# Decode attention over a 512 MiB cache: K and V loaded by pairs of heads instead of single heads

## The chip, the cores and the metric

The kernel runs on one core of a Trainium2 chip. The metric is the device time of one execution in microseconds. A core has TensorE (PE, matrix products into PSUM), VectorE (DVE), ScalarE (ACT), GpSimd (POOL) and SyncE (SP), which issues most transfers here. A transfer (DMA) is issued by SP or ACT and carried out by 16 DMA engines, each of which takes its share of the rows. The engines run on their own and wait for each other through semaphores. SBUF has 128 partitions; a transfer into it writes one row into each.

## What is computed

One token for each of four batch entries goes through an attention block with a stored cache and then a gated MLP:

```
x: [4, 1, 512] bf16            h  = x + Attn(layernorm(x))
k_cache, v_cache: [4, 32, 8192, 128] bf16   (256 MiB each)
q = (x @ wq) per head          wq: [512, 4096]
p = softmax(q . k / sqrt(128)) over 8192 keys
o = p . v                      wo: [4096, 512]
h2 = h + (sigmoid(g) * u) @ w_down,  g = ln(h) @ w_gate,  u = ln(h) @ w_up   (F = 1792)
```

There are 4 x 32 = 128 (batch, head) pairs, called heads here. Each reads 2 MiB of K and 2 MiB of V once. All inputs together are 550.8 MB.

## The kernel before

**Loading.** `KV` holds NSL = 8 slots, each of 64 x 128 bf16 values per partition: 16 KB per partition, 2 MiB in all. `k_src` and `v_src` give partition p the 64 consecutive keys 64p to 64p + 63 of one head, so a row of a transfer is 16 KB. The list `order` (L321 to L331) says which load follows which: K of head 0 in four pieces (128 rows of 4 KB), the query weights in four pieces (rows of 8 KB), then K heads; four pieces of the output weights (rows of 1 KB) come between K 2 and K 5, and from head 9 on K n and V n - 9 alternate (LAGH = 9). The gate weights stand before V of head 125, the up and down weights at the end. The last V is in four pieces again. All loads are issued by SP in this order. `take_slot` gives slots in turn; SP waits until the load that held the slot is used up: for K until its last transpose (`t_tr`), for V until its last product (`t_pv`). `pump` issues a load as soon as that point has been written into the program.

**Scores.** K arrives with keys on partitions and must be turned. A head is worked in four chunks of 16 keys per partition. For each chunk, `transposes` (L369) turns 32x32 blocks of 32-bit words on DVE into one of NKT = 4 buffers `kTc`, and `scores` (L383) runs four matmuls of 512 columns against `Lq`, a window that holds the head's query so that its scores land on their own rows of a PSUM bank. `q_windows` fills such windows from `q2`. Eight heads (GH = 8) times four chunks times four fill the 128 rows of one bank: a group, of which there are 16.

**Softmax.** When a group's scores are complete, `softmax` (L400) takes the row maximum on DVE, and hands four steps, p1 to p4, to the list `chain`. They find each head's maximum, take the exponent on ACT with a running sum, divide, and write the probabilities into `PT` with a 32x32 transpose on DVE. They are written into the program at fixed distances, so that other work stands between them.

**Output.** `pv` (L445) has the probabilities as the stationary 32 columns and V as the moving 512, four matmuls on four column strips at once, summed in a bank per group. `finish` (L498) copies the bank to SBUF on ACT, picks the wanted strips by four matmuls against `selq`, and `project` (L482) multiplies by the output weights and adds to the residual `sth`. The last group is worked otherwise: V is stationary and the moving operand is one column, 512 small matmuls (L473), so that no selection follows.

**Order of work.** The main loop (L553) counts chunks u. At each it writes the transposes of chunk u, due steps of `chain`, the scores of chunk u - 1, and one chunk of `pv` 36 chunks back, so that PE alternates four score matmuls with four output matmuls. `q_projection` (L520) stands after the first four transposes and has one step for each piece of the query weights.

**The end.** After the last `pv` come the projection, the second layernorm, gate and up products (L597), the sigmoid, the down product in two halves (L613), a transpose back and the store of 4 KB.

```
for n in range(NH):
    order.append((4 * n, 0, "k", n))
    order.append((4 * (n + LAGH), 1, "v", n))
```

Of the kernel before, what the change touches and what calls it, by code (L numbers as in the profile page):

```python
# [11 lines left out]
NSL = 8  # L12
NKT = 4
LAGH = 9
GH = 8

# [60 lines left out]
def bass_sequential_preLN__mha_block_cached__glu_gated_glu__decode_kernel(  # L77
# [18 lines left out]
    R = S // 128  # L96
    NK = R // 4
    RC = R // 4
    QH = 2
    NH = B * H  # L100
    NG = NH // GH
    SCALE = float(DH) ** -0.5
# [6 lines left out]
    with ExitStack() as es:  # L109
# [21 lines left out]
        Lq = SB("Lq", [128, 2, QH, 4, W], BF16)  # L131
# [3 lines left out]
        PT = SB("PT", [128, 2, NK * GH * 32], BF16)  # L135
# [37 lines left out]
        keys = ["sp", "act", "dve", "pool", "pe", "x", "out", "wg", "wu", "wd0", "wd1"]  # L173
        keys += [f"sl{i}" for i in range(NSL)] + [f"k0p{i}" for i in range(4)] + [f"vl{i}" for i in range(4)]
        keys += [f"wq{i}" for i in range(4)] + [f"wo{i}" for i in range(4)]
# [13 lines left out]
        t_lq0 = emit("pool", lambda e: e.memset(Lq[:, :, :, :, :], 0.0))  # L189
# [3 lines left out]
        t_x = prog.dma("sp", "x", lambda e: e.dma_start(x_bf[:, :], A_x.rearrange("b s d -> (b s) d")))  # L193
# [30 lines left out]
        def f_xT(e):  # L224
            ins = None
            for c in range(NDC):
                ins = e.matmul(cols(bank[XO], c), x_bf[:, 128 * c:128 * (c + 1)], ident[0:B, 0:B],
                               start=True, stop=True)
            return ins
        t_xT = emit("pe", f_xT, [t_x, t_ident])  # L230
        t_xTc = emit("dve", lambda e: e.tensor_copy(stx[:, 0:NDC * B], bank[XO][:, 0:NDC * B]), [t_xT])
        t_h = emit("dve", lambda e: e.tensor_copy(sth[:, 0:NDC * B], bank[XO][:, 0:NDC * B]), [t_xT])
        t_xn, t_xst = layernorm(stx, t_xTc, 0, xnT, bank[XS], None)
        t_m8 = emit("dve", lambda e: e.tensor_reduce(
            M8[:, :], identf[:, :].rearrange("p (t i) -> p i t", i=GH), AX.X, ALU.max), [t_identf])
# [3 lines left out]
            Gmat[:, :].rearrange("p (t i) -> p t i", i=GH),  # L239
            bass.AP(raw(M8), 0, [[GH, 128], [0, 16], [1, GH]])), [t_m8])  # L240
# [15 lines left out]
        sp_jobs = []  # L256

        def k_src(n):
            b, h = n % B, n // B
            return A_k_cache[b, h, :, :].rearrange("(p r) d -> p (r d)", p=128)  # L260

        def v_src(n):
            b, h = n % B, n // B
            return A_v_cache[b, h, :, :].rearrange("(p r) d -> p (r d)", p=128)

        QN = R * 128 // 4
# [20 lines left out]
        def emit_head(kind, n, src, done, pieces):  # L287
            slot, w = take_slot((kind, n))
            if pieces:
                done[n] = [prog.dma("sp", f"{pieces}{s}", lambda e, s=s: e.dma_start(  # L290
                    KV[:, slot, QN * s:QN * (s + 1)], src[:, QN * s:QN * (s + 1)]), w) for s in range(4)]
                return
            done[n] = [prog.dma("sp", f"sl{slot}", lambda e: e.dma_start(KV[:, slot, :], src), w)] * 4  # L293

        def emit_weight(kind):
            slot, w = take_slot((kind, 0))
            if kind == "wd":
                wd_v = in_slot(slot, [[D, NFT], [1, D]])
                src = B_w_down.rearrange("(t p) f -> p t f", p=128)
                half = NFT // 2  # L300
                t_w[kind] = (wd_v, [prog.dma("sp", f"wd{i}", lambda e, i=i: e.dma_start(
                    wd_v[:, half * i:half * (i + 1), :], src[:, half * i:half * (i + 1), :]), w) for i in range(2)])
                return
# [4 lines left out]
        def emit_wq():  # L308
            src = A_wq.rearrange("(c p) f -> p c f", p=128)
            for c in range(NDC):  # L310
                t_wq.append(prog.dma("sp", f"wq{c}", lambda e, c=c: e.dma_start(wq_v[:, c, :], src[:, c, :])))  # L311
# [4 lines left out]
        def emit_wo(i):  # L316
            src = A_wo.rearrange("(h p) f -> p h f", p=128)
            t_wo.append(prog.dma("sp", f"wo{i}", lambda e: e.dma_start(  # L318
                wo_v[:, 8 * i:8 * (i + 1), :], src[:, 8 * i:8 * (i + 1), :]), [t_qproj[0]]))

        order = []  # L321
        for n in range(NH):
            order.append((4 * n, 0, "k", n))
            order.append((4 * (n + LAGH), 1, "v", n))
        order.sort()
        order = [(k, n) for _, _, k, n in order]
        order.insert(1, ("wq", 0))
        for i, after in enumerate((2, 3, 4, 5)):
            order.insert(order.index(("k", after)) + 1, ("wo", i))
        order.insert(order.index(("v", NH - 3)), ("wg", 0))  # L330
        order += [("wu", 0), ("wd", 0)]  # L331
# [8 lines left out]
        def pump():  # L340
            while next_dma[0] < len(order) and ready(*order[next_dma[0]]):
                kind, n = order[next_dma[0]]
                next_dma[0] += 1
                if kind == "k":
                    emit_head("k", n, k_src(n), t_k, "k0p" if n == 0 else "")
                elif kind == "v":
                    emit_head("v", n, v_src(n), t_v, "vl" if n == NH - 1 else "")
                elif kind == "wq":
                    emit_wq()
                elif kind == "wo":  # L350
                    emit_wo(n)
                else:
                    emit_weight(kind)
# [15 lines left out]
        def transposes(n, s):  # L369
            u = 4 * n + s  # L370
            slot = slot_of["k", n]
            t_copy[u] = emit("dve", lambda e: e.transpose(  # L372
                kTc[:, u % NKT, :], KVW[:, slot, 64 * RC * s:64 * RC * (s + 1)]), [t_k[n][s], t_score.get(u - NKT)])
            if s == 3:
# [5 lines left out]
        def scores(u):  # L380
            n, s = u // 4, u % 4
            g, i = n // GH, n % GH
            first = i == 0 and s == 0  # L383
            last = i == GH - 1 and s == 3
            off = 31 - (GH * s + i)
            k3 = kTb[:, u % NKT, :].rearrange("p (r c i e) -> p r c i e", c=2, i=32, e=2)

            def f(e):
                ins = None
                for ce in range(4):  # L390
                    ins = e.matmul(sbank(g), Lq[:, n // QH % 2, n % QH, ce, off:off + 128],  # L391
                                   k3[:, :, ce // 2, :, ce % 2], start=first and ce == 0, stop=last and ce == 3)
                return ins
            w = [t_copy[u], t_lq[n // QH]]
# [6 lines left out]
        def softmax(g):  # L401

            t_mx = emit("dve", lambda e: e.tensor_reduce(mpart[:, :], sbank(g), AX.X, ALU.max),  # L403
                        [t_score[32 * g + 31], st_.get("p1")])
            box = {}

            def p1():
# [5 lines left out]
                    mrow[0:1, :], bank[XS][0:1, 0:128].rearrange("p (k i) -> p i k", i=GH), AX.X, ALU.max),  # L413
                    [box["p1"]])
                box["d2"] = emit("dve", lambda e: e.tensor_copy(  # L415
                    rowpad[0:1, :].rearrange("p (k i) -> p k i", i=GH),
                    bass.AP(raw(mrow), 0, [[GH, 1], [0, 16], [1, GH]])), [d2, t_rp0])
# [19 lines left out]
            def p4():  # L437
                pb = g % 2
                dst = bass.AP(raw(PT), pb * NK * GH * 32, [[2 * NK * GH * 32, 128], [GH * 32, NK], [1, 4], [36, GH]])
                t_ptc[g] = emit("dve", lambda e: e.transpose(dst, E_sb[:, :]),  # L440
                                [box["d4"], t_pt0, t_pvg.get(g - 2)])
            return [(4, p1), (6, p2), (9, p3), (13, p4)]

        def pcol(g, i, rr):
            return g % 2, (rr * GH + i) * 32  # L445

        def pv(n, m):
            g, i = n // GH, n % GH
            first = i == 0 and m == 0
            last = i == GH - 1 and m == 3  # L450
            slot = slot_of["v", n]
            w = [t_v[n][m], t_ptc[g]]
            if first and g > 1:
                w.append(t_oev[g - 2])
            if g < NG - 1:
                def f(e):
                    mms = []
                    for j in range(4):
                        rr = 4 * m + j
                        pb, o = pcol(g, i, rr)  # L460
                        mms.append(e.matmul(obank(g)[32 * j:32 * (j + 1), :], PT[:, pb, o:o + 32],  # L461
                                            in_slot(slot, [[RC * 128, 4], [1, 128]], rr * 128),
                                            start=first, stop=last, tile_position=(0, 32 * j)))
                    return mms if last else mms[-1]
                tok = emit("pe", f, w, incs=4 if last else 1)
            else:
                def f(e):
                    ins = None
                    for r in range(16 * m, 16 * (m + 1)):
                        q = r // RC  # L470
                        pb, o = pcol(g, i, r % RC)
                        o += 4 * i + q
                        ins = e.matmul(obank(g)[:, i:i + 1], KV[:, slot, 128 * r:128 * (r + 1)],  # L473
                                       PT[:, pb, o:o + 1], start=(r == 0), stop=(r == R - 1))
                    return ins
                tok = emit("pe", f, w)
            if m == 3:
# [20 lines left out]
        def finish(g):  # L498
# [5 lines left out]
            def s1():  # L504
                def f(e):
                    ins = None
                    for q in range(4):
                        ins = e.matmul(bank[XO][:, 0:GH], O_sb[:, 128 * q:128 * (q + 1)],  # L508
                                       selq[:, q:q + 29:4], start=(q == 0), stop=(q == 3))
# [8 lines left out]
            return [(4, s1), (6, s2)]  # L518

        def q_projection():  # L520
            for c in range(NDC):
                def f(e, c=c):
                    ins = None
# [4 lines left out]
                    return ins  # L528
                t = emit("pe", f, [t_wq[c], t_xn, t_xTc])
# [12 lines left out]
            q_windows(0)  # L542
            q_windows(1)

        def q_windows(k):
            dst = bass.AP(raw(Lq), k % 2 * QH * 4 * W + 31, [[2 * QH * 4 * W, 128], [4 * W, QH], [W, 4], [32, 4]])
            src = bass.AP(raw(q2), QH * k, [[4 * NH, 128], [1, QH], [NH, 4], [0, 4]])
            keep = bass.AP(raw(amask), 0, [[4, 128], [0, QH], [0, 4], [1, 4]])
            t_lq[k] = emit("dve", lambda e: e.tensor_tensor(dst, src, keep, ALU.mult),  # L549
                           [st_["q"], t_lq0, t_am, t_score.get(4 * QH * (k - 1) - 1)])  # L550


# [128 lines left out]
```

## Time and profile before

| | us |
|---|---|
| median of 3 runs | 1307.28 (1306.99 to 1307.47) |
| the profiled execution | 1307.25 |
| its span in the profile | 1305.1 |
| PE busy (matmul) | 883.7 |
| DVE busy | 682.3 |
| ACT busy | 27.4 |
| DMA, mean over the span | 423 GB/s |
| issue to landing, K head | 33.9 |
| DVE's waits for K | 445.1 |

The profile is of one execution. Busy times are sums over instructions; a share of the span is not a share of the path. "PE" lines are matmuls and "PEld" the loads of their stationary operand; "SPq" is SP's issuing of a transfer. The slices cut the span into 40 equal parts with one digit of busy share each. In a list of waits a line says who waited, for whom, the sum in us, how often, and the longest. In a timeline a line says start, duration, engine, line of the kernel, operation, what it writes and reads, how many, and in brackets how long the engine had been idle and what released it.

### The profile page before, as it was taken

To read this page: it belongs to the slowest core of one execution; us is meant where nothing else is said; L and a number is where in the kernel's file an instruction comes from. 1 tells how busy PE (TensorE), PEld (TensorE's weight loads), DVE (VectorE), ACT (ScalarE), POOL (GpSimd) and SP (SyncE) were. 2 spreads that over 40 slices of the span, in tenths; PEclk is the share of its full clock that TensorE was granted. 3 is DMA by queue.
4 is the path that set the end of the run, shared out by engine and by line. 5 is a ranking of instruction groups with operands and counts; after the bars stand their busy time and mean duration, and the time that the engine had idled before them with its cause. 6 is when DMAs were issued, how large, how long until landed. Compare 5 with 4: busy or idle time off the path is not lost.

```text
span 1305.1 us, 11528 instructions
## 1 busy us (share of the span) xinstructions
PE 883.7 (68%) x5133; PEld 283.5 (22%) x5133; DVE 682.3 (52%) x750; ACT 27.4 (2%) x55; POOL 10.3 (1%) x11
## 2 busy tenths in 40 slices
PE   4675776777667676676677667676667767667654
PEld 2121221222112121221212112121221212112133
DVE  6675554645546555554645546554554645545420
ACT  0000000000000000000000000000000000000000
POOL 3000000000000000000000000000000000000000
PEclk9888788787888888788888888888888888888865
DMA  9999999999999999999999999999999999999997
GB/s 373 407 426 428 428 427 427 427 428 428 427 430 426 428 429 427 427 428 427 428 427 428 429 427 429 426 428 428 426 429 429 425 429 428 427 428 426 428 423 306
DMA packets 45433, 551.52 MB, mean 423 GB/s; under 512 B 4420, under 2 KB 10312, under 8 KB 12360
## 3 DMA queue, kind: packets, MB, share of 16 engines
q1 hardware_dynamic: 45384, 550.79, 99.8%
q8 instruction: 40, 0.66, 0.2%
q14 instruction: 9, 0.07, 0.0%
HBM read 550.77 MB, written 0.00 MB: 422 GB/s over the span
## 4 chain that ended last, share of the span: by engine, by line
DMA 84%; PE 13%; SPq 2%; DVE 0%; issue 0%
DMA KV<-in_A_v_cache_dram 80%; PE PS L391 9%; PE PS L461 4%; DMA KV<-in_A_k_cache_dram 1%; DMA KV<-in_B_w_down_dram 1%; SPq L293 1%; DMA Wreg<-in_A_wq_dram 1%; SPq L318 0%; DVE kTc L372 0%; SPq L311 0%; SPq L290 0%; PE PS L473 0%; PE PS L525 0%; PE PS L613 0%; SPq L193 0%
## 5 line engine op out<-in xcount | busy, mean ns | idle before, releaser
L372 DVE STREAM_TRANSPOSE kTc<-KV 128x1024 f32<-128x1024 f32 x512 | 606.1, 1225 | 446.0 <-DMA KV<-in_A_k_cache_dram 445.1
L391 PE MATMUL PS<-kTc,Lq 128*128 128x512 bf16 x2048 | 650.8, 448 | 14.5 <-DVE kTc L372 12.6
L461 PE MATMUL PS<-KV,PT 128*32 128x512 bf16 x1920 | 224.4, 458 | 335.0 <-DMA KV<-in_A_v_cache_dram 335.0
L391 PEld LDWEIGHTS PS<-kTc,Lq 128*128 128x128 bf16 x2048 | 181.4, 109 | 330.1 <-issue 209.1
L461 PEld LDWEIGHTS PS<-KV,PT 128*32 128x32 bf16 x1920 | 50.2, 95 | 594.8 <-DMA KV<-in_A_v_cache_dram 386.9
L549 DVE TENSOR_TENSOR Lq<-q,amask 128x32 bf16<-128x32 bf16 x64 | 18.1, 285 | 41.1 <-PE PS L391 40.8
L440 DVE STREAM_TRANSPOSE PT<-E_sb 128x512 bf16<-128x512 bf16 x16 | 37.3, 2333 | 0.0
L425 ACT ACTIVATE E_sb<-PS,negmb 128x512 bf16<-128x512 f32 x16 | 11.0, 688 | 1153.8 <-DVE negmb L423 1153.8
L473 PE MATMUL PS<-PT,KV 128*128 128x1 bf16 x512 | 15.2, 165 | 20.1 <-DMA KV<-in_A_v_cache_dram 19.9
L508 PE MATMUL PS<-selq,O_sb 128*128 128x8 f32 x120 | 16.7, 266 | 11.7 <-ACT O_sb L500 11.7
L412 DVE TENSOR_REDUCE mrow<-PS 1x8 f32<-1x128 f32 x16 | 4.4, 276 | 31.8 <-PE PS L408 31.8
L508 PEld LDWEIGHTS PS<-selq,O_sb 128*128 128x128 f32 x120 | 15.3, 200 | 16.6 <-ACT O_sb L500 16.6
L473 PEld LDWEIGHTS PS<-PT,KV 128*128 128x128 bf16 x512 | 14.4, 104 | 20.8 <-DMA KV<-in_A_v_cache_dram 20.6
L585 DVE CAST OT<-PS 128x8 bf16<-128x8 f32 x1 | 0.2, 167 | 35.0 <-PE PS L473 35.0
L420 PE MATMUL PS<-identf,rowpad 128*128 128x1 f32 x32 | 8.1, 322 | 10.5 <-DVE rowpad L415 10.5
L403 DVE TENSOR_REDUCE mpart<-PS 128x1 f32<-128x512 f32 x16 | 10.9, 683 | 7.2 <-PE PS L391 7.2
L433 DVE RECIPROCAL rsum<-PS 128x1 f32<-128x1 f32 x16 | 2.7, 168 | 21.8 <-PE PS L431 21.8
L525 PE MATMUL PS<-xnT,Wreg 128*128 128x4 bf16 x128 | 4.0, 167 | 12.8 <-DMA Wreg<-in_A_wq_dram 12.8
L500 ACT ACTIVATE O_sb<-PS 128x512 f32<-128x512 f32 x15 | 9.0, 597 | 73.7 <-PE PS L461 73.7
L420 PEld LDWEIGHTS PS<-identf,rowpad 128*128 128x128 f32 x32 | 6.7, 261 | 16.6 <-DVE rowpad L415 16.6
L431 PEld LDWEIGHTS PS<-sig,Gmat 128*128 128x128 f32 x32 | 7.9, 305 | 7.6 <-issue 6.1
L431 PE MATMUL PS<-sig,Gmat 128*128 128x1 f32 x32 | 9.0, 351 | 0.7 <-ACT E_sb L425 0.7
(66 smaller groups left out, 97.2 us busy)
## 6 DMA issues: line engine op xcount, KB each, us to landing
KV<-in_A_k_cache_dram SPq DMA_DIRECT2D x127, 2048.0 KB, 33.9
KV<-in_A_v_cache_dram SPq DMA_DIRECT2D x127, 2048.0 KB, 33.3
Wreg<-in_A_wq_dram SPq DMA_DIRECT2D x4, 1024.0 KB, 11.8
Wreg<-in_A_wo_dram SPq DMA_DIRECT2D x4, 1024.0 KB, 15.0
KV<-in_A_k_cache_dram SPq DMA_DIRECT2D x4, 512.0 KB, 5.7
KV<-in_A_v_cache_dram SPq DMA_DIRECT2D x4, 512.0 KB, 27.5
KV<-in_B_w_gate_dram SPq DMA_DIRECT2D x1, 1792.0 KB, 34.5
KV<-in_B_w_up_dram SPq DMA_DIRECT2D x1, 1792.0 KB, 26.0
```

The lines of the kernel that those rows point to most:

```text
L293: done[n] = [prog.dma("sp", f"sl{slot}", lambda e: e.dma_start(KV[:, slot, :], src), w)] * 4
L372: t_copy[u] = emit("dve", lambda e: e.transpose(kTc[:, u % NKT, :], KVW[:, slot, 64 * RC * s:64 * RC * (s + 1)]), [t_k[n][s], t_score.get( ...
L391: ins = e.matmul(sbank(g), Lq[:, n // QH % 2, n % QH, ce, off:off + 128], k3[:, :, ce // 2, :, ce % 2], start=first and ce == 0, stop=last ...
L403: t_mx = emit("dve", lambda e: e.tensor_reduce(mpart[:, :], sbank(g), AX.X, ALU.max), [t_score[32 * g + 31], st_.get("p1")])
L420: t = emit("pe", lambda e: e.matmul(bank[XS][:, 128:129], rowpad[:, :], identf[:, 0:1], start=True, stop=True), [box["d2"], t_rp0])
L425: box["a2"] = emit("act", lambda e: e.activation(E_sb[:, :], sbank(g), ACT.Exp, bias=negmb[:, 0:1], scale=SCALE, accum_out=sig[:, 0:1]), [ ...
L431: t = emit("pe", lambda e: e.matmul(bank[XS][:, 130:131], Gmat[:, :], sig[:, 0:1], start=True, stop=True), [box["a2"], t_gm])
L440: t_ptc[g] = emit("dve", lambda e: e.transpose(dst, E_sb[:, :]), [box["d4"], t_pt0, t_pvg.get(g - 2)])
L461: mms.append(e.matmul(obank(g)[32 * j:32 * (j + 1), :], PT[:, pb, o:o + 32], in_slot(slot, [[RC * 128, 4], [1, 128]], rr * 128), start=fir ...
L473: ins = e.matmul(obank(g)[:, i:i + 1], KV[:, slot, 128 * r:128 * (r + 1)], PT[:, pb, o:o + 1], start=(r == 0), stop=(r == R - 1))
L508: ins = e.matmul(bank[XO][:, 0:GH], O_sb[:, 128 * q:128 * (q + 1)], selq[:, q:q + 29:4], start=(q == 0), stop=(q == 3))
L549: t_lq[k] = emit("dve", lambda e: e.tensor_tensor(dst, src, keep, ALU.mult), [st_["q"], t_lq0, t_am, t_score.get(4 * QH * (k - 1) - 1)])
```

## The change

K and V of two neighbouring heads of one batch entry are loaded by one transfer: the 128 rows are 2 heads x 64 rows, and a row is 128 consecutive keys, 32 KB. `KV` has four slots of 4 MiB instead of eight of 2 MiB. There are 64 such pairs. A pair is worked in eight chunks; half of the partitions belong to one head and half to the other, and the index layouts of the score rows, of `M8`, `Gmat`, `Lq`, `PT` and the selection follow from that. A group is four pairs, still eight heads, and there are still 16 groups.

The order of loads is written anew. The query weights come first, as one transfer with rows of 32 KB (input row 4p + c on partition p, and x is turned with the matching stride, in addition to the old way for the residual); then K of pair 0 in four pieces, K 1, the output weights in one transfer, K 2, K 3, and from there K n + 4 and V n in turn; the last V in two pieces; then gate, up and down weights, the down weights in three pieces of 8, 4 and 2 tiles. x is loaded through ACT's queue.

The order on the engines follows the same list `steps`: all eight chunks of a K pair, then all eight of a V pair, with the steps of `chain` counted by chunks. The query projection stands before all of it. The last group is worked like the others, and PT is written by two transposes of 64 partitions for each group.

```diff
-NSL = 8
+NSL = 4
 NKT = 4
-LAGH = 9
+NLQ = 4
+LAGP = 4
 GH = 8
+GP = 4
+WDT = (0, 8, 12, 14)
...
-        t_x = prog.dma("sp", "x", lambda e: e.dma_start(x_bf[:, :], A_x.rearrange("b s d -> (b s) d")))
+        t_x = prog.dma("act", "x", lambda e: e.dma_start(x_bf[:, :], A_x.rearrange("b s d -> (b s) d")))
...
+        def kv_src(cache, n):
+            b, h = n % GP, 2 * (n // GP)
+            return cache[b, h:h + 2, :, :].rearrange("h (p r) d -> (h p) (r d)", p=64)
...
+        def emit_pair(kind, n, cache, done, pieces, cut):
             slot, w = take_slot((kind, n))
+            src = kv_src(cache, n)
+            if cut > 1:
+                q = R * 128 // cut
                 done[n] = [prog.dma("sp", f"{pieces}{s}", lambda e, s=s: e.dma_start(
-                    KV[:, slot, QN * s:QN * (s + 1)], src[:, QN * s:QN * (s + 1)]), w) for s in range(4)]
+                    KV[:, slot, q * s:q * (s + 1)], src[:, q * s:q * (s + 1)]), w) for s in range(cut)]
                 return
-            done[n] = [prog.dma("sp", f"sl{slot}", lambda e: e.dma_start(KV[:, slot, :], src), w)] * 4
+            done[n] = [prog.dma("sp", f"sl{slot}", lambda e: e.dma_start(KV[:, slot, :], src), w)]
...
         def emit_wq():
-            src = A_wq.rearrange("(c p) f -> p c f", p=128)
-            for c in range(NDC):
-                t_wq.append(prog.dma("sp", f"wq{c}", lambda e, c=c: e.dma_start(wq_v[:, c, :], src[:, c, :])))
+            src = A_wq.rearrange("(p c) f -> p (c f)", p=128)
+            t_wq.append(prog.dma("sp", "wq", lambda e: e.dma_start(Wreg[:, :], src)))
...
+        steps = [("k", n) for n in range(LAGP)]
+        for n in range(NP):
+            if n + LAGP < NP:
+                steps.append(("k", n + LAGP))
+            steps.append(("v", n))
+        order = [("wq", 0), *steps, ("wg", 0), ("wu", 0), ("wd", 0)]
+        order.insert(order.index(("k", 1)) + 1, ("wo", 0))
...
-                t_ptc[g] = emit("dve", lambda e: e.transpose(dst, E_sb[:, :]),
-                                [box["d4"], t_pt0, t_pvg.get(g - 2)])
-            return [(4, p1), (6, p2), (9, p3), (13, p4)]
+                w = [box["d4"], t_pt0, t_pvg.get(g - 2)]
+                for z in range(2):
+                    dst = bass.AP(raw(PT), 64 * z * 2 * PTW + pb * PTW + 4 * z,
+                                  [[2 * PTW, 64], [128, 2 * RC], [1, 4], [40, GP]])
+                    t_ptc[g] = emit("dve", lambda e, z=z, dst=dst: e.transpose(dst, E_sb[64 * z:64 * z + 64, :]), w)
+            return [(1, p1), (3, p2), (6, p3), (8, p4)]
...
+        q_projection()
+        pump()
+        for kind, n in steps:
+            for m in range(NCH):
+                u = NCH * n + m
+                if kind == "k":
+                    transposes(n, m)
+                    advance()
+                    scores(u)
...
+                else:
+                    advance()
+                    pv(u)
+                    if m == NCH - 1 and n % GP == GP - 1:
+                        chain += [(tick[0] + d, fn) for d, fn in finish(n // GP)]
+                pump()
...
-        gl = NG - 1
-        t_ot = emit("dve", lambda e: e.tensor_copy(OT[:, gl % 2, :], obank(gl)[:, 0:GH]),
-                    [t_pvg[gl], st_["ot"][gl % 2]])
-        project(gl, t_ot)
...
-        for i in range(2):
+        for i in range(len(WDT) - 1):
```

## The prediction

> **What bounds the kernel now.** I read the page's slices and queues first, then its chain, then windows and the timeline at both ends.
>
> ```profile
> DMA  9999999999999999999999999999999999999997
> GB/s 373 407 426 428 428 427 427 427 428 428 427 430 426 428 429 427 427 428 427 428 427 428 429 427 429 426 428 428 426 429 429 425 429 428 427 428 426 428 423 306
> ...
> q1 hardware_dynamic: 45384, 550.79, 99.8%
> ...
> DMA 84%; PE 13%; SPq 2%; DVE 0%; issue 0%
> ```
>
> The DMA engines are full in 39 of 40 slices and move about 428 GB/s. PE is busy 68% of the span and DVE 52%, so an engine matters only if it lets the transfer queue run dry.
>
> ```profile
> SPq L293 <- DVE kTc L372: 611.2, 122, 11.9
> SPq L293 <- PE PS L461: 494.5, 119, 7.1
> ```
>
> SP's waits are for slots, yet they cost nothing: the page's list of DMA issues has 33.9 us from the issue of a K head to its landing, and at 428 GB/s one head of 2,097,152 bytes takes 4.900 us. So nearly seven of the eight slots are queued at the DMA engines while one is consumed. The time is bytes over rate, plus the two ends.
>
> Next, whether the rate depends on the length of a row. A transfer always has 128 rows. The windows (their last two columns are the DMA share and GB/s) give 16 KB rows; PE's waits for the query weights at the start give 8 KB rows; the pieces of the last V head give 4 KB rows:
>
> ```profile
> 100.00:600.00 500.00, 345.64 (x1764) 103.60 (x1764) 264.79 (x284) 8.26 (x18) 0.00 (x0) 0.84 1.01 428
> ```
>
> ```profile
> 12.21 1.01 PE L525 MATMUL PS<-xnT,Wreg 128*128 128x4 bf16 x32 [8.35 <-DMA Wreg<-in_A_wq_dram]
> ...
> 19.69 1.01 PE L525 MATMUL PS<-xnT,Wreg 128*128 128x4 bf16 x32 [1.49 <-DMA Wreg<-in_A_wq_dram]
> ...
> 1289.49 0.58 PE L473 MATMUL PS<-PT,KV 128*128 128x1 bf16 x16 [0.25 <-DMA KV<-in_A_v_cache_dram]
> ...
> 1292.01 0.59 PE L473 MATMUL PS<-PT,KV 128*128 128x1 bf16 x16 [0.65 <-DMA KV<-in_A_v_cache_dram]
> ...
> 1301.51 0.91 PE L613 MATMUL PS<-hhT,KV 128*128 128x4 bf16 x28 [1.24 <-DMA KV<-in_B_w_down_dram]
> ```
>
> Each line starts when a piece lands. Three pieces of 8 KB rows between 12.21 and 19.69 are 2.493 us each; two pieces of 4 KB rows between 1289.49 and 1292.01 are 1.26 us each; 16 KB rows take 4.900. From 8 to 16 KB the slope is 2.407 per 8 KB, which leaves 0.09 us fixed per transfer; from 4 to 16 KB it is 0.303 per KB, which leaves 0.047; from 4 to 8 KB it leaves 0.03. The last fenced line shows the end: the last half of the down weights lands at 1301.5, and only then does PE do the last 28 matmuls.
>
> **The change, part by part.**
>
> 1. *Pairs in 32 KB rows.* Before there are 254 whole heads, 8 quarter heads and 4 query-weight pieces: 266 transfers of 128 rows. After: 126 whole pairs, 4 + 2 pieces, 1 for the query weights: 133. The bytes are the same, so 133 fixed costs go. The bounds are 133 x 0.03 = 4.0 and 133 x 0.09 = 12.0 us, and below them nothing, if a 32 KB row is cut in two inside. A loss is not excluded: the lowest rate of a full stream here is 402 GB/s (20 to 60 us, where the output weights' 1 KB rows mix in), and at 402 the 536.9 MB of K and V would take 1335.5 instead of 1254.4 us, 81 more. I take 0.07, between the two estimates that use the 16 KB rows, since those are nearest to 32 KB: 9.3 us. All of it is on the path, as the DMA engines never rest.
>
> [...]
>
> 2. *Query weights first.* SP issues them as its first DMA at 0.74 where it now issues x; K's first piece is at 1.14. The stream starts 0.4 us earlier: -0.4. x moves to ACT's queue, whose other work there is a table load of 1.28 us; x lands by about 4, and its layernorm (2.61 to 5.12 now) is done by 8. The 4 MiB land at about 1.7 + 9.8 = 11.5, so x is covered. PE then does all 128 matmuls in 4 x 1.01 us instead of only the last 32 after the last landing; scores start near 19 instead of 22.8. This is hidden either way: at 19 SP has queued the first two pairs and the output weights, which last beyond 40 us. The output weights' DMA waits for those matmuls (about 16) with two K pairs behind it on SP; the queue then holds work until 31. It is one DMA instead of four with the same 1 KB rows: nothing.
>
> 3. *Four slots of 4 MiB.* A slot's next transfer must be issued before the three other slots drain, 3 x 9.73 = 29 us after the slot's landing. A K pair is freed by its eighth transpose: 8 x 1.23 = 9.8 us when DVE sets the pace, 8 x 1.82 = 14.6 when the scores run at the slow clock. A V pair is 8 x 0.55 = 4.4 us, after at most that K work. Both leave over 9 us even when they come one after the other, so the waits stay free: 0. What is late next would be SP, never the engines.
>
> 4. *Softmax by groups of four pairs; PT written by two transposes of 64 partitions.* DVE gets up to 16 x 2.33 = 37.3 us more if 64 partitions cost what 128 do, on an engine that waits 445 us for K. A group's chain delays the next K pair by about 5 us, within the 9: 0. The windows of q are the same 64 operations.
>
> 5. *The end.* Now wg precedes the last V heads; after, wg, wu and wd all follow. From the last V landing (1291.96) to the last wd landing (1301.46) is now 9.5 us; wg adds about what wu takes (4.5), so 14.0. The compute from that landing to hhT takes 1292.01 to 1299.29, 7.3 us now; it gains three more PV chunks' worth (4 x 0.55 - 0.59 = 1.6), the O_sb copy (0.9 with its read) and the selection matmuls (1.9): 11.7. wd takes 4.96 us for 14 tiles, 0.354 each, so its pieces land at 11.9, 13.3 and 14.0. The 32 + 16 matmuls (28 take 0.91) end at 12.8 and 13.8; then 8 matmuls, 0.26, follow the last landing instead of 28, 0.91: -0.65. The cover is thin, 0.2 us; were it gone, the end would slip by what is missing. The slots of wu and wd are freed by the PVs of two pairs before the last, 5 us before that landing. The Sqrt table load (1.28) now comes behind the O_sb copy and fits beside the selection matmuls.
>
> 6. *Instructions.* 512 PV matmuls of one column become 128 of 512; the page's instruction queue (40 fetches of 0.66 MB) shrinks by about three. These fetches share the DMA engines. In the last 5 us (1296.5 to 1301.5) the DMA share is only 0.49, so some engines finish later than others and the latest sets the end. I cannot price this; ±2 us, taken as 0.
>
> Sum: 9.3 + 0.4 + 0.65 = 10.35 us. The profiled execution took 1307.25 (span 1305.1 and 2.15 around it), 0.03 under the median: 1296.9.
>
> [...]
>
> **The rivals.**
>
> *Longer rows give nothing* (the fixed cost is per byte, or a 32 KB row travels as two of 16). For it: 4 to 8 KB rows show only 0.03. Against: 8 to 16 KB show 0.09. Time: 1307.25 - 0.4 - 0.65 = 1306.2.
>
> *A larger gain*: the fixed cost is above what the slopes show. At twice 0.07 it is 18.6, and with the two ends 1287.6. For it: nothing but the scatter of the three estimates (0.03 to 0.09); against: all three lie below it.
>
> *PE becomes the bound* (slower). Place: the block of 8 score chunks and 8 PV chunks of a pair. At the slow clock this is 14.6 + 4.4 = 19.0, and the softmax and the output step add about 6.3 us per four pairs (PE 0.63 + 0.59 + 0.59 + 1.87 + 0.38, DVE and ACT between them 2.2): 20.5. It decides from 19.5, the DMA time of two pairs' loads. If the clock stayed slow: 19 + 64 x 20.5 + 17 = 1348. For it: a V block waits behind the K block, and PE idles between blocks. Against:
>
> ```profile
> 602.46 0.62 PE L461 MATMUL PS<-KV,PT 128*32 128x512 bf16 x4 [4.49 <-DMA KV<-in_A_v_cache_dram]
> 603.01 1.89 PE L391 MATMUL PS<-kTc,Lq 128*128 128x512 bf16 x4
> ...
> 609.31 1.05 PE L391 MATMUL PS<-kTc,Lq 128*128 128x512 bf16 x4
> ```
>
> After 6 us of unbroken work four score matmuls fall from 1.89 to 1.05, so a PE that is late runs faster.
>
> **How the numbers follow.** Forecast (1291 to 1303) 0.70; no gain from rows (1303 to 1307) 0.12; larger gain (below 1291) 0.06; slower, PE bound 0.09 and a lower rate 0.03. The range 1290 to 1304.5 takes in the forecast with part of its two neighbours. About 0.2%, 2.6 us, is what a measurement of this kernel tells from no change: faster 0.77, same 0.11, slower 0.12.
>
> **What would show it.** Right: q1's packets fall from 45,384 to below 27,000; the steady slices read 430 to 432; the chain still rests on V's landings; the last landing is followed by 8 matmuls. Wrong: slices below 428 in the middle or a DMA digit under 9 (slots or PE); packets near 45,000 (rows cut); a gap between the last wd landing and its matmuls.

## The result and the profile after

The changed kernel takes 1295.26 us (median of 4 runs, 1295.08 to 1295.30) against 1307.26 (1306.99 to 1307.47): 12.0 us less, a ratio of 0.9908 with a 95% interval of 0.9891 to 0.9925. The forecast was 1296.9 in a range from 1290 to 1304.5. The profiled execution took 1295.28, its span 1293.4.

The page of the changed kernel: DMA share and rate in the 40 slices, the packets of the load queue, and the chain by engine.

```profile
DMA  9999999999999999999999999999999999999997
GB/s 394 408 429 435 427 433 432 427 434 430 430 431 430 433 429 432 429 433 429 429 436 429 429 433 427 435 428 430 435 426 434 428 433 434 424 435 431 428 432 306
...
q1 hardware_dynamic: 26192, 550.78, 99.5%
...
DMA 76%; DVE 22%; SPq 1%; PE 1%; issue 0%
```

The DMA engines are as full as before, and the slices lie near 431 instead of 428. Packets, of which each row of K or V is one, fell from 45,384 to 26,192 for the same bytes. The windows say it with less scatter (last two columns: DMA share and GB/s):

```profile
100.00:600.00 500.00, 312.35 (x1784) 122.12 (x1782) 280.02 (x290) 8.25 (x18) 0.00 (x0) 0.78 1.00 431
600.00:1240.00 640.00, 403.28 (x2266) 158.24 (x2266) 365.22 (x376) 11.00 (x24) 0.00 (x0) 0.78 1.00 431
```

The next two views are the list of waits (who waited for whom: sum, times, longest) and the list of DMA issues (last column: us from issue to landing):

```profile
SPq L295 <- DVE kTc L367: 939.9, 64, 21.4
SPq L295 <- PE PS L458: 214.6, 59, 8.2
```

```profile
KV<-in_A_k_cache_dram SPq DMA_DIRECT2D x63, 4096.0 KB, 29.7
KV<-in_A_v_cache_dram SPq DMA_DIRECT2D x63, 4096.0 KB, 34.5
```

SP waits longer than before for slots and it costs nothing: a load is issued 29.7 us before it lands, and its own 4 MiB need 9.73 at 431 GB/s. The chain now runs through K and the transposes that free its slots, where before it ran through V. The first line is the chain by line before, the second after:

```profile
DMA KV<-in_A_v_cache_dram 80%; PE PS L391 9%; PE PS L461 4%; DMA KV<-in_A_k_cache_dram 1%; DMA KV<-in_B_w_down_dram 1%; SPq L293 1%; DMA Wreg<-in_A_wq_dram 1%; SPq L318 0%; DVE kTc L372 0%; SPq L311 0%; SPq L290 0%; PE PS L473 0%; PE PS L525 0%; PE PS L613 0%; SPq L193 0%
DMA KV<-in_A_k_cache_dram 72%; DVE kTc L367 22%; DMA KV<-in_A_v_cache_dram 2%; DMA Wreg<-in_A_wq_dram 1%; SPq L302 1%; DMA KV<-in_B_w_down_dram 1%; PE PS L458 0%; PE PS L511 0%; PE PS L597 0%; SPq L318 0%; PE PS L604 0%; DVE o_sb L606 0%; DVE h2T L602 0%
```

The figures fit each other: a slot comes round every 4 x 9.73 = 38.9 us, for K 29.7 + 9.2 of transposes, for V 34.5 + 4.4 of products. K's slot leaves the least time between issue and landing, and the chain goes that way. The wait in the DMA engines' queue lies inside both figures.

The two ends, from the timeline of PE (start, us, engine, line, what, count, and in brackets the idle time before and what ended it):

```profile
13.34 3.57 PE L511 MATMUL PS<-xnT,Wreg 128*128 128x4 bf16 x128 [8.85 <-DMA Wreg<-in_A_wq_dram]
...
1276.40 1.90 PE L458 MATMUL PS<-KV,PT 128*32 128x512 bf16 x16 [3.03 <-DMA KV<-in_A_v_cache_dram]
...
1284.20 3.15 PE L582 MATMUL PS<-hnT,KV 128*128 128x4 bf16 x112 [1.31 <-DVE hnT L223]
1288.33 0.99 PE L597 MATMUL PS<-hhT,KV 128*128 128x4 bf16 x32 [0.98 <-DMA KV<-in_B_w_down_dram]
1289.67 1.07 PE L597 MATMUL PS<-hhT,KV 128*128 128x4 bf16 x24 [0.35 <-DMA KV<-in_B_w_down_dram]
```

The last piece of the down weights lands at 1290.32, inside the last line, before its last 8 matmuls. So the whole gain of 12.0 splits in this way, by the landing records of the two traces: the first 24 MiB (eight heads of K and the query and output weights) land at 65.41 instead of 66.77 (1.36); from there to the last landing the stream takes 1224.9 instead of 1234.7 (9.8); from the last landing to the end 3.08 instead of 3.64 (0.56); outside the span 1.88 instead of 2.15 (0.27).

### The profile page after: what moved, and what is told of

It reads as the page before. It is cut to its first block, busy times and chain, and to the rows that moved or that the text cites. A ratio compares the mean times of both kernels' runs of the same rounds, so it can differ in the third digit from the quotient of the medians.

```text
span 1293.4 us, 10558 instructions
## 1 busy us (share of the span) xinstructions
PE 800.3 (62%) x4761; PEld 318.5 (25%) x4761; DVE 720.8 (56%) x766; ACT 28.0 (2%) x56; POOL 10.3 (1%) x11
## 3 DMA queue, kind: packets, MB, share of 16 engines
q1 hardware_dynamic: 26192, 550.78, 99.5%
## 4 chain that ended last, share of the span: by engine, by line
DMA 76%; DVE 22%; SPq 1%; PE 1%; issue 0%
DMA KV<-in_A_k_cache_dram 72%; DVE kTc L367 22%; DMA KV<-in_A_v_cache_dram 2%; DMA Wreg<-in_A_wq_dram 1%; SPq L302 1%; DMA KV<-in_B_w_down_dram 1%; PE PS L458 0%; PE PS L511 0%; PE PS L597 0%; SPq L318 0%; PE PS L604 0%; DVE o_sb L606 0%; DVE h2T L602 0%
## 5 line engine op out<-in xcount | busy, mean ns | idle before, releaser
L386 PE MATMUL PS<-kTc,Lq 128*128 128x512 bf16 x2048 | 618.8, 462 | 429.7 <-DVE kTc L367 425.0
L367 DVE STREAM_TRANSPOSE kTc<-KV 128x1024 f32<-128x1024 f32 x512 | 587.7, 1211 | 346.2 <-DMA KV<-in_A_k_cache_dram 345.7
L386 PEld LDWEIGHTS PS<-kTc,Lq 128*128 128x128 bf16 x2048 | 215.7, 113 | 809.5 <-DVE kTc L367 539.5
L458 PE MATMUL PS<-KV,PT 128*32 128x512 bf16 x2048 | 139.5, 400 | 22.6 <-DMA KV<-in_A_v_cache_dram 13.7
L439 DVE STREAM_TRANSPOSE PT<-E_sb 64x512 bf16<-64x512 bf16 x32 | 78.4, 2450 | 1.0
L535 DVE TENSOR_TENSOR Lq<-q,amask 128x16 bf16<-128x16 bf16 x64 | 14.2, 229 | 85.9 <-PE PS L386 85.9
L494 PEld LDWEIGHTS PS<-selq,O_sb 128*128 128x128 f32 x128 | 30.7, 332 | 7.4 <-issue 4.4
L494 PE MATMUL PS<-selq,O_sb 128*128 128x8 f32 x128 | 27.7, 345 | 0.8 <-ACT O_sb L486 0.8
L403 PE MATMUL PS<-identf,mpart 128*1 128x128 f32 x32 | 6.1, 271 | 13.8 <-DVE mpart L398 13.8
L476 PEld LDWEIGHTS PS<-OT,Wreg 128*128 128x128 bf16 x128 | 6.9, 113 | 9.1 <-issue 7.9
L427 PEld LDWEIGHTS PS<-sig,Gmat 128*128 128x128 f32 x32 | 4.8, 187 | 12.1 <-ACT E_sb L421 11.9
## 6 DMA issues: line engine op xcount, KB each, us to landing
KV<-in_A_k_cache_dram SPq DMA_DIRECT2D x63, 4096.0 KB, 29.7
KV<-in_A_v_cache_dram SPq DMA_DIRECT2D x63, 4096.0 KB, 34.5
```

The source lines that it names most:

```text
L367: t_copy[u] = emit("dve", lambda e: e.transpose(kTc[:, u % NKT, :], KVW[:, slot, 64 * RC * s:64 * RC * (s + 1)]), [t_k[n][s * len(t_k[n]) ...
L386: ins = e.matmul(sbank(g), Lq[:, n % NLQ, ce, off:off + 128], k3[:, :, ce // 2, :, ce % 2], start=first and ce == 0, stop=last and ce == 3)
L427: t = emit("pe", lambda e: e.matmul(bank[XS][:, 130:131], Gmat[:, :], sig[:, 0:1], start=True, stop=True), [box["a2"], t_gm])
L439: t_ptc[g] = emit("dve", lambda e, z=z, dst=dst: e.transpose(dst, E_sb[64 * z:64 * z + 64, :]), w)
L476: ins = e.matmul(cols(bank[XO][:, 64:64 + NDC * B], c), wo_v[:, h, 128 * c:128 * (c + 1)], OT[:, ob, B * hh:B * (hh + 1)], start=(hh == 0) ...
L535: t_lq[n] = emit("dve", lambda e: e.tensor_tensor(dst, src, keep, ALU.mult), [st_["q"], t_lq0, t_am, t_score.get(NCH * (n - NLQ + 1) - 1)])
```

## The experiments

The theory: each row of a transfer costs a DMA engine a fixed few nanoseconds beside its bytes, and the change halves the rows; slots, PE and DVE have spare. Rivals: the cost is per transfer; the gain comes from the order of loads or the end; fewer instructions are fetched. Since the predicted time was right, the runs were to show whether it was right for the predicted reason.

**Two transfers for a pair**, each of 128 rows of 16 KB:

```diff
-            done[n] = [prog.dma("sp", f"sl{slot}", lambda e: e.dma_start(KV[:, slot, :], src), w)]
+            q = R * 128 // 2
+            done[n] = [prog.dma("sp", f"sl{slot}{'ab'[s]}", lambda e, s=s: e.dma_start(
+                KV[:, slot, q * s:q * (s + 1)], src[:, q * s:q * (s + 1)]), w) for s in range(2)]
...
```

> The changed kernel with every whole pair loaded by two transfers of 128 rows of 16 KB (two semaphores for a slot); slots, order, ends and compute as in the changed kernel. Theory: the gain of 12 us is mostly the fixed cost that a row has, so with 16 KB rows again some 126 x 0.07 to 0.08 = 9 to 10 us come back: 1304 to 1305 us, steady slices near 428 GB/s. Rival, the new order, slots and ends make the gain: 1295 to 1296.5. Rival, the cost is one of the transfer (its completion) and not of the row: 1304 to 1305 too, which the run with one transfer and cut rows tells apart.

1304.86 us (1304.70 to 1305.14), 9.6 more than the changed kernel, ratio to the kernel before 0.9983 (0.9974 to 0.9993). The windows are back at 428. All else of the change (slots, order, groups, end) is still in it and is worth 2.2 us.

**One transfer for a pair, each row cut in two.** The halves of a row go to two places in SBUF, so that a transfer has 256 rows of 16 KB:

```diff
+            done[n] = [prog.dma("sp", f"sl{slot}", lambda e: e.dma_start(
+                bass.AP(raw(KV), slot * q, [[KVROW, 128], [NSL * q, 2], [1, q]]),
+                src.rearrange("p (a f) -> p a f", a=2)), w)]
...
```

> The changed kernel with one transfer for each pair, but the two halves of a row go to two places of the slot region, so that each partition gets two runs of 16 KB; number of transfers, slots, order and compute as in the changed kernel. Theory, a fixed cost for each row: 126 more rows of 16 KB on each of 8 rows of an engine, 1303 to 1305 us (about 1 us less than with two transfers, whose completions are saved). Rival, a fixed cost for each transfer: 1295 to 1296. Rival, order and ends: 1295 to 1296.

1304.52 (1304.35 to 1304.74). The page counts packets, and the window the rate:

```profile
DMA packets 42372, 551.45 MB, mean 423 GB/s; under 512 B 2260, under 2 KB 8152, under 8 KB 9176
```

```profile
100.00:600.00 500.00, 310.13 (x1784) 121.04 (x1782) 280.43 (x290) 8.25 (x18) 0.00 (x0) 0.78 1.01 428
```

As many transfers as in the changed kernel, and yet nearly the whole loss, 9.3 us for 126 x 8 = 1008 more rows on each DMA engine, 9.2 ns a row: the cost is the row's, and the transfer's own is the remaining 0.3 us, at the edge of what the runs tell apart.

**The stream by itself**, at four row lengths and from half of the partitions; SP's loads are the whole kernel:

```
# (elements in a row, partitions of one transfer, slots, transfers)
PHASES = ((4096, 128, 16, 96), (8192, 128, 8, 48), (16384, 128, 4, 24),
          (24576, 128, 3, 16), (16384, 64, 8, 48))
```

> Loads alone, no attention and no MLP: five stretches of 96 MiB of the cache each, in transfers of 128 rows of 8 KB, 16 KB, 32 KB, 48 KB, and of 64 rows of 32 KB into one half of the partitions. A slot is loaded again as soon as it has landed. The output is zeros. Theory, a fixed cost of about 0.07 us for the 8 rows that each engine has in a transfer: periods of 2.48, 4.89, 9.71 and 14.53 us, so 423, 429, 432 and 433 GB/s. Rival, the cost is in proportion to the bytes: the same rate, 428 to 432, in all four. For 64 rows of 32 KB: 432 GB/s if only rows count, less if half of the partitions take less.

The windows of its five stretches, from one run:

```profile
20.00:230.00 210.00, 0.00 (x0) 0.00 (x0) 1.00 1.01 422
260.00:470.00 210.00, 0.00 (x0) 0.00 (x0) 1.00 1.01 428
500.00:700.00 200.00, 0.00 (x0) 0.00 (x0) 1.00 1.00 432
730.00:940.00 210.00, 0.00 (x0) 0.00 (x0) 1.00 1.00 434
980.00:1420.00 440.00, 0.00 (x0) 0.00 (x0) 1.00 1.00 208
```

With no engine computing, rows of 8, 16, 32 and 48 KB give 422, 428, 432 and 434 GB/s: the two kernels' rates are those of their rows. The last line missed its expectation: transfers of 64 rows into one half of the partitions, alternating halves, run at half the rate, 208 GB/s against 432, with the engines shown as fully busy. Whether the turns between the halves do it, or rows into one half are as slow by themselves, was not shown: no run loaded one half alone.

**Fewer slots.**

```diff
-NSL = 4
+NSL = 3
```

> The changed kernel with three slots of 4 MiB instead of four. Theory (step 3 of the prediction: a slot is freed long before the other slots drain): with three slots 2 x 9.73 = 19.5 us are left; a K pair is freed about 9.2 us after it lands, 13 to 14 at the start of a group: 1295 to 1297 us. Rival, four slots are just enough and the slot waits are near the path: 1300 us or more, DMA digits under 9 in the middle slices.

1295.30 (1295.12 to 1295.54). K is issued 25.8 and V 20.0 us before landing, still over twice the 9.73 of a pair. The fourth slot is worth nothing. Then two slots, with the gate and the down weights in one of them together:

```diff
-NSL = 4
+NSL = 2
...
-                wd_v = in_slot(slot, [[D, NFT], [1, D]])
+                slot, w = slot_of["wg", 0], []
+                wd_v = in_slot(slot, [[D, NFT], [1, D]], 64 * 128)
...
```

> The changed kernel with two slots of 4 MiB (the down weights share the slot of the gate weights). Theory: with two slots only 9.73 us are left from a landing to the next issue, against 9.2 us until a K pair is freed, 13 to 14 at the start of a group, and about 1 to 2 us from an issue to the first bytes; the DMA engines run dry at most K pairs, for 0.5 to 3 us, and 5 us at each of 16 groups: 1390 us, between 1340 and 1450, with DMA digits of 8 and 9. Rival, a slot wait costs nothing at any number of slots: 1295.

1492.52 in one run, above the expected range of 1340 to 1450. The DMA engines do run dry here: window of the steady part, and a part of the chain (start, us, what):

```profile
600.00:1240.00 640.00, 345.33 (x1946) 135.82 (x1946) 311.12 (x322) 9.63 (x21) 0.00 (x0) 0.73 0.88 368
```

```profile
749.94 12.20 DMA KV<-in_A_k_cache_dram
762.14 0.03 issue
762.16 9.14 DVE kTc L368 x8
771.31 0.02 issue
771.33 13.29 DMA KV<-in_A_k_cache_dram
```

Every pair of K goes through load, transposes, load with no other K queued ahead: 21 to 25 us a pair against 19.46 of DMA time. The mechanism is the expected one and its size was not: the load takes 12 to 14 us from its issue, not 9.7. V's rows may stand between; that was not tested.

**The two ends.** Down weights in two pieces of 7 tiles instead of 8, 4 and 2; then, in another run, K of pair 0 ahead of the query weights, as before the change, with x on SP:

```diff
-WDT = (0, 8, 12, 14)
+WDT = (0, 7, 14)
```

> The changed kernel with the down weights in two pieces of 7 tiles, as before, instead of 8, 4 and 2. Theory (step 5): 28 matmuls, 0.9 us, follow the last landing instead of 8, 0.26: 1295.9 us (+0.5 to +0.8). Rival, the compute before it ends last anyway: 1295.3.

```diff
-        t_x = prog.dma("act", "x", lambda e: e.dma_start(x_bf[:, :], A_x.rearrange("b s d -> (b s) d")))
+        t_x = prog.dma("sp", "x", lambda e: e.dma_start(x_bf[:, :], A_x.rearrange("b s d -> (b s) d")))
-        order = [("wq", 0), *steps, ("wg", 0), ("wu", 0), ("wd", 0)]
+        order = [steps[0], ("wq", 0), *steps[1:], ("wg", 0), ("wu", 0), ("wd", 0)]
```

> The changed kernel with x issued by SP as the first DMA and the four pieces of the first K pair ahead of the query weights, as before. Theory (step 2): the stream of large transfers starts 0.4 us later and nothing else changes: 1295.7 us. Rival, the place of the query weights matters for the start beyond that (scores start later, slots are freed later): 1296.5 or more. Rival, nothing: 1295.3.

1295.83 (1295.70 to 1295.99), 0.57 more, and 1295.62 (1295.43 to 1295.67), 0.36 more. In the second the scores start at 30.12 instead of 20.32, and these 9.8 us cost next to nothing. The run changes two things at once, and in its trace (of an execution of 1295.43) the last landing is at 1290.35, 0.03 later than in the changed kernel's; so where the 0.36 comes from is not shown.

**More instructions to fetch.** 2048 extra matmuls of one column into an unused bank, four behind each chunk's scores:

```diff
+                for _ in range(4):
+                    ins = e.matmul(bank[UBK][:, 0:1], ident[:, :], ident[:, 0:1], start=True, stop=True)
...
```

> The changed kernel with four more matmuls of one column on each of 512 chunks, into a bank that is used only at the end. They add 4096 instructions to the 10,558, so some 16 fetches of 16 KB to the 37 of the instruction queue, and less than 0.5 us of PE time to each chunk, which PE has free. Theory (step 6, left unpriced there): fetches run on the same DMA engines and make some of them late, and the latest sets the end; the last 8 us, in which only part of the engines still move data, grow by 16/37: 1298 to 1299 us. Rival, fetches cost nothing: 1295.3.

1298.32 (1298.27 to 1298.34), 3.0 more, though PE has spare and the windows stay at 431. The page shows 16 fetches more than the 37 of the changed kernel:

```profile
q8 instruction: 53, 0.87, 0.3%
```

The last landing moves from 1290.32 to 1293.31, about 0.19 us for each more fetch of 16 KB. By bytes alone 16 fetches would be 0.26 MB, 0.6 us at 431 GB/s. The landing records show where the rest lies: a transfer is counted as landed by 16 marks, and of those of the first half of the last V the earliest comes 0.17 us later than in the changed kernel (1263.47 against 1263.30), the latest 2.98 (1274.41 against 1271.43). So some engines fall behind and the end follows them, not the mean of 16. That they are those which the fetches fell on is argued; the records do not name the engine.

**The changed kernel again**, on the chip of the next run:

> The changed kernel again, beside the next one on the same chip: 1295.3 us.

1295.33 (1295.23 to 1295.41).

**Long rows for the last weights too**: gate and up in rows of 14 KB, and what the strided reading then needs; among it a second residual tile of 64 bytes per partition ahead of `KV`, and K of pair 0 uncut.

```diff
...
+            sto = SB("sto", [128, NDC * B], FP32)
-                src = B_w_down.rearrange("(t p) f -> p t f", p=128)
+                src = B_w_down.rearrange("(p t) f -> p t f", p=128)
-            src = (B_w_gate if kind == "wg" else B_w_up).rearrange("(c p) f -> p c f", p=128)
+            src = (B_w_gate if kind == "wg" else B_w_up).rearrange("(p c) f -> p c f", p=128)
-                        ins = e.matmul(bk[:, B * t:B * (t + 1)], wv[:, c, 128 * t:128 * (t + 1)],
+                        ins = e.matmul(bk[:, B * t:B * (t + 1)], wv[:, c, t:t + NFT * 127 + 1:NFT],
...
```

> A version that should beat both: the changed kernel with long rows for the weights of the MLP too (gate and up weights 14 KB instead of 3.5 KB, down weights 8, 4 and 2 KB in place of 1 KB rows), for which the second layernorm works on a second copy of the residual with the other order of columns; the first K pair in one transfer. Theory, fewer rows: some 0.3 us less for each of the gate and up weights, 0.6 or more for the down weights, 0.2 for the first pair; of the 1.3 at the end nearly all shows, as the compute from the last V landing takes 11.3 us to the hidden vector and 12.3 to the end of the first down matmuls, against 12.6 for the transfers: 1293.9 us. Rival, loading stationary operands with a stride of 28 bytes is slower on PE and the compute ends last: 1295 us or more.

1292.58 (1292.48 to 1292.77): faster, but not for the expected reason. Timeline of PE at the end, and the first steady window:

```profile
1271.19 1.90 PE L463 MATMUL PS<-KV,PT 128*32 128x512 bf16 x16 [3.84 <-DMA KV<-in_A_v_cache_dram]
...
1279.04 6.88 PE L598 MATMUL PS<-hnT,KV 128*128 128x4 bf16 x112 [1.31 <-DVE hnT L227]
1286.29 1.66 PE L613 MATMUL PS<-hhT,KV 128*128 128x4 bf16 x56 [0.38 <-DVE hhT L605]
```

```profile
100.00:600.00 500.00, 309.62 (x1830) 121.85 (x1827) 280.48 (x295) 8.25 (x18) 0.00 (x0) 0.79 1.00 433
```

The gate and up products take 6.88 us instead of 3.15 with a strided stationary operand, and PE now ends last; that is a loss. But the last V, which lies ahead of all these weights, starts its products at 1271.19 instead of 1276.40: the whole stream had become faster, 433. In the trace's records of single packets its 32 KB packets took 1213 ns nearly all, where the changed kernel has 1215 and 1222 mixed. The 64 bytes had moved `KV` from byte 28,352 of a partition to byte 28,416. So the next runs did that alone, in both kernels:

```diff
         sth = SB("sth", [128, 2 * NDC * B], FP32)
+        pad = SB("pad", [128, NDC * B], FP32)
```

> The changed kernel with 64 unused bytes per partition ahead of KV, which moves KV from byte 28,352 to byte 28,416 of each partition, a multiple of 256, and changes nothing else. In the run with long weight rows, which had the same shift, 32 KB packets took 1215.1 ns in the mean (nearly all 1213) instead of 1218.7 (1215 and 1222 mixed). Theory (the place of KV does it): 3.6 ns less for each of about 1016 packets per DMA engine, 3.7 us: 1291.6 us, steady windows 432 to 433 GB/s, packets at 1213. Rival (the long weight rows or the uncut first pair did it): 1295.3 and 1215/1222 as before.

> The kernel before with the same 64 bytes ahead of KV, same shift to byte 28,416. Its 16 KB packets take 616.1 ns in the mean (613 and 620 mixed). Theory (the cost of the odd place is per row, whatever its length): some 4.5 ns less for each of about 2035 packets per engine, 9.2 us: 1298.1 us, packets at 611 to 612, steady windows 430 to 431. Then the gain of the change at this place of KV is only 6.5 us instead of 12.0: about half of what I have put down to the row's length is the place of the buffer, paid once per row. Rival A (the cost of the place is per byte): 3.7 us less, 1303.4, and the gain of longer rows stays near 12. Rival B (no effect): 1307.1.

| | as it was, KV at byte 28,352 | KV at byte 28,416 | gain |
|---|---|---|---|
| kernel before | 1307.29 (1306.74 to 1307.41) | 1297.40 (1297.17 to 1297.55) | 9.9 |
| its 16 KB packets, mean | 616.1 ns | 612.2 ns | 3.9 ns |
| changed kernel | 1295.33 (1295.23 to 1295.41) | 1289.65 (1289.52 to 1289.70) | 5.7 |
| its 32 KB packets, mean | 1218.7 ns | 1214.9 ns | 3.8 ns |
| the change | 12.0 | 7.75 | |

Ratios to the kernel before: 0.9925 (0.9913 to 0.9938) for the kernel before with its buffer moved, 0.9866 (0.9851 to 0.9881) for the changed one. The steady windows, first of the kernel before and then of the changed one with the buffer moved:

```profile
100.00:600.00 500.00, 345.86 (x1778) 103.54 (x1779) 265.84 (x285) 8.25 (x18) 0.00 (x0) 0.85 1.01 431
```

```profile
100.00:600.00 500.00, 312.66 (x1782) 122.63 (x1780) 279.64 (x289) 8.25 (x18) 0.00 (x0) 0.78 1.00 433
```

The times expected were 1298.1 and 1291.6. The rows became 3.9 ns shorter at 16 KB and 3.8 at 32 KB: the cost of the place goes with the row, not with the byte, as the theory had it, and the kernel with twice the rows gained more. (Both gained more than that times the rows of an engine, 7.9 us for 2032 rows and 3.9 for 1016; some other packets are shorter too, those of gate and up 140.5 ns instead of 144.4. How the rest comes to be at the end is open.) The 64 bytes also move the tiles behind `KV`; no run moved `KV` alone. The stream by itself, whose buffer begins at byte 16,512, shows that the mix needs no work on other tiles: it computes nothing, and its 32 KB packets were mixed again, 1213 to 1221 ns.

Not every row pays. In the changed kernel 1045 of the 16,256 rows of 32 KB took 1213 ns, as nearly all did in the run with long weight rows, at byte 28,416; in the run with two slots, whose `KV` also begins at 28,352, 12,894 of 16,256 did. So the start at 28,352 cost time in the runs whose transfers stayed queued, and most rows paid nothing in the one whose DMA engines ran dry. By what mechanism was not shown, nor what other starts cost: these two places alone were compared.

The changed kernel with its buffer moved, 1289.65 us, is the fastest of all.

## Why the prediction was right, and where it was not

1. *Pairs in 32 KB rows: -9.3 us forecast, about -10.2 measured* (the 11.14 of the landings less 0.36 for part 2 and 0.6 for part 6, which are both less sure). The place is right: undoing this part alone returned 9.6 of the 12.0. The step's unit is wrong. It priced a transfer at 0.07 us; the run with cut rows shows that a row pays. Its size was near: 0.07 for a transfer of 8 rows on each engine is 8.75 ns a row, and the cut rows cost 9.2.

   The packets say the same when the starts of the rows are compared. Their durations give 2 x 616.1 - 1218.7 = 13.5 ns, which is too much: the record of a row mostly begins 3 to 4 ns before the one ahead of it on its engine ends, and two short rows count this twice. From 100 to 1240 us the starts lie 613.75 and 1218.03 ns apart in the mean, so a row costs 2 x 613.75 - 1218.03 = 9.5 ns. With the buffer moved they lie 609.47 and 1213.09 apart, and 5.9 ns remain. The landings agree: from the first 24 MiB to the last landing the change gains 9.8 us as it was, and 5.7 with the buffer moved in both kernels.

   That 0.07 came so near is partly luck. It was a choice among slopes of 0.03 to 0.09, and they could not tell two costs apart that both go with the row: the 5.9 ns that stay with the buffer at byte 28,416 and what the start at 28,352 adds, on half as many rows after the change. Of the 12.0 us of this change, 7.75 are there at 28,416, and 4.25 are an accident of where the buffer began. Neither the step nor the rivals had looked at that address.

   Over a mean engine the packet durations fell by 15.4 us, and the last landing moved by 11.1. The overlap of the records, 3 to 4 ns for each of 1064 rows fewer on an engine, is most of the difference.

2. *Query weights first: -0.4 forecast, -0.36 by the run that undid it,* though its last landing moved by 0.03 only. They landed at 13.3, not 11.5, and scores began at 20.3, not 19; hidden, as said, and hidden even at 30.

3. *Four slots: 0 forecast, 0 measured.* K was freed 9.2 us after landing in the steady part and 13.75 at a group's start, against the bounds 9.8 and 14.6. Three slots are as good. But the forecast that the chain would still rest on V failed: it runs through K, whose slot is held 4.8 us longer than V's.

4. *The two transposes into `PT`.* 37.3 us more were allowed for, at equal cost of 64 and 128 partitions; it was 41.1, since the smaller one, which also writes in another pattern, takes even more (before 2333 ns, 16 times):

   ```profile
   L439 DVE STREAM_TRANSPOSE PT<-E_sb 64x512 bf16<-64x512 bf16 x32 | 78.4, 2450 | 1.0
   ```

   It was free, as said. The rival of PE as the bound had a point of decision of 19.5 us a pair; DMA share 1.00 in the windows shows that it was never reached, at a granted clock of 0.78.

5. *The end: -0.65 forecast, -0.56 measured.* 8 matmuls follow the last landing, as said. hhT was done 11.3 us after the last V landing, forecast 11.7, and the pieces landed at 11.8, 13.2 and 13.9, forecast 11.9, 13.3 and 14.0. So the cover was 0.5 us and not 0.2. Two pieces instead of three cost 0.57.

6. *Instruction fetches: taken as 0 within 2 us.* An estimate exists now: about 0.19 us each, so 0.6 us for the three fewer of the changed kernel. The sum was 1.65 short of 12.0: 0.9 of part 1, this 0.6, and 0.27 outside the span, less 0.13 in parts 2 and 5.

Of the rivals, "longer rows give nothing" fell with the windows (428 to 431). A lower rate, to which the prediction gave 0.03, did not appear between rows of 16 and 32 KB: it rose.

## What to carry to other kernels

Where the DMA engines are full, count rows, not transfers: each row of these streams cost an engine 5.9 ns beside its bytes when the buffer started at byte 28,416 of a partition, and 9.5 at byte 28,352, so look at the start address of every large buffer before its layout is worked over; 64 bytes of padding gave 9.9 us where the whole rewrite gave 12.0. When you read how a fixed cost goes with the number of packets, take the distance between their starts, since their durations overlap. Read what a deeper queue is worth from the time between issue and landing: here, above twice the transfer's own time, a slot fewer cost nothing; with two slots, at 12 to 14 us against 9.7, it cost 15%. When a run surprises, compare the durations of single packets: a mean rate of 431 or 433 shows little, 1215 and 1222 against 1213 showed where to look.

## What was not expected of the hardware

- The start of the destination in SBUF: 3.8 to 3.9 ns a row in the mean, 9.9 us in the kernel before; yet at the same start, byte 28,352, most rows of the run with two slots took 1213 ns.
- Transfers of 64 rows into half of the partitions: 208 GB/s with the two halves in turn, at a DMA share of 1.00.
- Sixteen more instruction fetches of 16 KB delayed the end by 3.0 us, about 0.19 each, five times what their bytes would at the full rate.
- A stationary operand with a stride of 28 bytes: 6.88 us for 112 matmuls instead of 3.15.
- A 32x32 block transpose of 64 partitions by 512 takes 2450 ns, one of 128 partitions 2333.
